# Next block's x loads, weight making and operand buffers moved between the up and down products of a Strassen-Winograd MLP pair

## The chip, the cores and the metric

The kernel runs on one core of one Trainium2 chip. The metric is the device time of one execution in microseconds (us), the median of several runs. A core has TensorE (PE: matmuls, and PEld: its weight loads), VectorE (DVE), ScalarE (ACT), GpSimd (POOL) and SyncE (SP); the last two issue nearly all DMAs here, POOL on the software queue q0, SP on the hardware queue q1.

## The reference

```
attn_out = retention(q, k, v)                      # 4 x 8 heads x 768 x 64
x = attn_out -> (3072, 512)
h = x @ w_in;  g = h * sigmoid(1.702 * h);  x = g @ w_out     # first MLP, 512 -> 2048 -> 512
h = x @ w_in2; r = max(h, 0); g = r * r;    x = g @ w_out2    # second MLP, same sizes
```

All in float32. Every operand of a big product is held as a high part and a low part (`hi`, `lo`), and a product is three matmuls: `lo*hi`, `hi*hi`, `hi*lo`.

## The kernel before

Retention comes first (24 units). Then the first MLP in its plain form for two token tiles of 512 (`for n in range(NSTD)`), and after that five *blocks* of 1024 tokens, in this order: (0, 1), which the code calls `plain`, (0, 2), (1, 0), (1, 1), (1, 2). The first number is the layer (0: first MLP, 1: second). A block has an *up* part (x times w_in) and a *down* part (g times w_out).

- The up part of `plain` is `up_plain`: 2 x 16 steps `f` of twelve matmuls, no Strassen. ScalarE applies the gelu from one of four PSUM banks (L809).
- The up part of the other blocks is `up2`: the seven products of Strassen-Winograd for each of eight `p`. An up step `p` is seven products of six matmuls each. Their results are copied (`copy`, L864, ScalarE), added (`add`, L869, VectorE) and put through gelu (layer 0) or the squared relu (layer 1: L891 and L892 on ScalarE for the quarter that needs no sum, L873 on VectorE for the three others). Products 6, 7 and 4 run on in the same PSUM bank, so each waits for the copy before it.
- The down part is `down2`: 28 steps `u` of twelve matmuls. Step u takes one operand `gx` (high and low part, made by `prepare`: L945 on ScalarE, L946 on VectorE), does one of the sums (L954, L957, L960) on g in its first twelve steps, and from step 12 on a piece (`tick`) of `x_operands`, which makes the next block's x operands (`xh`, `xl`, L702, L703). `prepare` runs two operands ahead; three pairs of tiles are used in turn, chosen by `k % 3`. Results leave through `copy` (L977), `add` (L980) and `store` (L972).

Weights of the blocks are read from DRAM (`kw`) by `fetch` (L764) on SP's queue, one tile `r` of 256 KB a product, into `SLOTS = 8` slots. Two of the slots exist early; six are opened in `up_plain` at step `f == NQ + 2` of its second half, where the pool `g` stood.

The Strassen weight combinations are made on the way by a generator, `maker`, of which `background(us)` runs pieces until their costs (the numbers that it yields) have used up the credit. A job of `make_second` loads 512 KB (`raw`, L272, POOL), scales it on ScalarE (L130, L131), joins and combines it on VectorE (L135 to L148, L377 to L381), casts it on ScalarE (L383), subtracts on VectorE (L345) and stores 896 KB (`kw<-wq`, L346, POOL). The costs of one job sum to 4.15. `later` holds a job's ScalarE pieces and its next load back until the next call of `background`. Credits: `BGK - 0.3 * c` a step of `up_plain` (c is its half), `BGUP` twice in an up step (not in the last p), `BGD` in each down step of layer 0.

The next block's x (`xb`, four tiles of 512 KB) is loaded on POOL's queue by `loads()`: in `up_plain` at `f == NQ - 2` of its second half, in `up2` at `p == NQ // 2`. POOL's queue runs in the order of the program; an xb load waits for its tile and for what stands ahead of it in that queue.

Of the kernel before, what the change touches and what calls it, by code (L numbers as in the profile page):

```python
# [11 lines left out]
F32R = mybir.dt.float32r  # L12
# [7 lines left out]
P = 128  # L20
# [6 lines left out]
NF = DFF // P  # L27
# [14 lines left out]
SLOTS = 8  # L42
EARLY = 2
BG = 4.7
BGK = 2.4
BGD = 0.35
CV0 = 12
RAWU = 7
FILL = 8
RAWS = 5  # L50
BGUP = 1.8

# [7 lines left out]
def tile_retention_then_two_ffns(  # L62
# [199 lines left out]

    raws = {}
    raw_p = []

    def load(n):
        if n < len(jobs):
# [58 lines left out]
    def make_second():  # L326

        with (
            tc.tile_pool(name="k3", bufs=1, side="right", reuse_waits="tile") as third,
            tc.tile_pool(name="k2", bufs=2, side="right", reuse_waits="tile") as pool,  # L330
        ):
            raw_p.append(third)
            load(2)
            hms = {}

            def scale(n):
                if n < len(jobs):
                    hm = raws[n][:, :, 1].bitcast(F32)
                    hms[n] = hm, later(lambda: scale_words(hm, raws[n]))

            def low(n, w, t, done):
                while not done:
                    yield None
                m, i = jobs[n]
                v.tensor_tensor(out=t[:, :, 1], in0=w[:, 1:8], in1=t[:, :, 0], op=ALU.subtract)  # L345
                nc.gpsimd.dma_start(  # L346
                    out=kw[1][m][i // 2][:, :, i % 2].rearrange("i p c -> p i c"),
                    in_=t.bitcast(F32).rearrange("p i h c -> p i (h c)"),
                )
                if i % 2:  # L350
                    made.add((1, m, i // 2))
                yield 1.1

            scale(0)
            last = None
            for n in range(len(jobs)):
                hm, done = hms.pop(n)
                while not done:
                    yield None
                scale(n + 1)  # L360
                raw = raws[n]
                hb = hm.bitcast(U32)
                w = pool.tile([P, 8, P], F32, tag="w", name=f"w32_{n}")
                wf = w.rearrange("p q c -> p (q c)")[:, 0:512]
                wu = wf.bitcast(U32)
                steps = join(wu, hb)
                next(steps)
                yield 0.45
                next(steps)
                yield 0.7  # L370
                round_up(wf, raw)
                later(lambda n=n: load(n + 3))
                yield 0.7
                if last is not None:
                    yield from low(*last)
                a21, a11, a12, a22, s1, s2, s3, s4 = (w[:, k] for k in range(8))
                v.tensor_tensor(out=s1, in0=a21, in1=a22, op=ALU.add)  # L377
                v.tensor_tensor(out=s3, in0=a11, in1=a21, op=ALU.subtract)
                yield 0.6
                v.tensor_tensor(out=s2, in0=s1, in1=a11, op=ALU.subtract)  # L380
                v.tensor_tensor(out=s4, in0=a12, in1=s2, op=ALU.subtract)  # L381
                t = pool.tile([P, 7, 2, P], F32R, tag="h", name=f"wq_{n}")
                done = later(lambda t=t, w=w: nc.scalar.copy(out=t[:, :, 0], in_=w[:, 1:8]))  # L383
                last = n, w, t, done
                yield 0.6
            yield from low(*last)
# [38 lines left out]
    hl = {}  # L425
# [15 lines left out]
    with tc.manual_schedule():  # L441
# [285 lines left out]
                lows.popleft()()  # L727
                yield

        def x_loads(l, n):  # L730
            return [load_block(f"xb{l}_{n}_{t}", (xkept, ykept)[l][2 * n + t]) for t in range(2)]


        plain = (0, NSTD // 2)
        blocks = [plain] + [(0, n) for n in range(NSTD // 2 + 1, NL)] + [(1, n) for n in range(NL)]
# [50 lines left out]
        ps_p = []  # L786
        banks = deque(range(8))

        def up_plain(loads):

            for n in range(NSTD, NSTD + 2):
                c = n - NSTD
                for f in range(NF):
                    hi, lo = weights(f, 0)
                    hp = hp_p.tile([P, TB], F32, tag="h", name=f"h{n}_{f}")
                    for k in range(KD):
                        xh, xl = hl[n][k]
                        nc.tensor.matmul(hp, lo[:, k], xh, start=(k == 0), stop=False)  # L798
                        nc.tensor.matmul(hp, hi[:, k], xh, start=False, stop=False)  # L799
                        nc.tensor.matmul(hp, hi[:, k], xl, start=False, stop=(k == KD - 1))  # L800
                    if c == 0 and f == 0:
                        down(NSTD - 1, NF - 1)
                        finish(NSTD - 1)
                        g_ctx.close()
                    r, p = divmod(f, NQ)
                    key = QS[2 * r + c], p // 2
                    if p % 2 == 0:
                        g[key] = (wa_p, wb_p)[c].tile([P, 2, TB], F32, tag="w1", name="g{}_{}".format(*key))
                    nc.scalar.activation(out=g[key][:, p % 2], in_=hp, func=ACTF.Gelu_apprx_sigmoid)  # L809
                    if c == 0 and f == 4:  # L810
                        split_x(n + 1, xs.pop(n + 1))
                    if c == 1:
                        if r == 1 and p > 0 and p % 2 == 0:
                            thirds(p // 2 - 1)
                        if f == NQ - 2:
                            loads()
                        if f in (NQ + 3, NQ + 5):
                            prepare(*plain)
                        if f == NQ + 2:
                            wr_p.extend(  # L820
                                ctx.enter_context(
                                    tc.tile_pool(name=f"wr{i}", bufs=1, side="left", reuse_waits="tile")
                                )
                                for i in range(EARLY, SLOTS)
                            )
                            fetch()
                    if f < NF - 1:
                        background(BGK - 0.3 * c)
            thirds(NQ // 2 - 1)
            first_ctx.close()  # L830
            ps_p.append(ctx.enter_context(tc.tile_pool(name="ps", bufs=1, space=PSUM, reuse_waits="tile")))
# [10 lines left out]
        def matmul(a, w, b, start, stop):  # L842
            nc.tensor.matmul(a, w, b, start=start, stop=stop, skip_group_check=True)  # L843

        def up2(l, n, first, loads):

            xb, yb, zb = {}, {}, {}
            late = deque()
# [19 lines left out]
            def add(t, a):  # L868
                v.tensor_tensor(out=t, in0=a, in1=t, op=ALU.add)  # L869
                if l == 0:  # L870
                    late.append(lambda: nc.scalar.activation(out=t, in_=t, func=ACTF.Gelu_apprx_sigmoid))
                else:
                    v.scalar_tensor_tensor(out=t, in0=t, scalar=0.0, in1=t, op0=ALU.max, op1=ALU.mult)  # L873

            for p in range(NQ + 1):
                if p == NQ // 2:
                    loads()
                if p < NQ:
                    xb[p] = bank(f"X{l}_{n}_{p}")
                    product(1, p, xb[p][0], True)  # L880
# [18 lines left out]
                        prepare(l, n)  # L899
                if p < NQ:  # L900
                    if (l, n) != blocks[-1] and p < NQ - 1:
                        background(BGUP)
                    yb = bank(f"Y{l}_{n}_{p}")
                    product(2, p, yb[0], True)
                    add(gt(11, p), yb[0])
# [6 lines left out]
                    copy(gt(22, p), xb[p][0])  # L912
                    add(gt(22, p), zb[p][0])
                    if (l, n) != blocks[-1] and p < NQ - 1:
                        background(BGUP)
                if p == NQ:
                    while late:
                        late.popleft()()
# [10 lines left out]
        def prepare(l, n):  # L929

            if not todo:
# [4 lines left out]
            hi, lo = (  # L936
                pool.tile([P, 2, TB], F32R, tag=tag, name=f"gx{l}_{n}_{i}_{m}_{e}")
                for e, (pool, tag) in enumerate(
                    ((wa_p, "w0"),) * 2 if k < 2 else
                    ((wa_p, "w0"), (wb_p, "w0")) if k % 3 == 1 else ((hl_p, "hl"),) * 2  # L940
                )
            )

# [15 lines left out]

                v.tensor_tensor(out=b11, in0=b22, in1=b11, op=ALU.subtract)  # L960

        def down2(l, n, tick):
            xb, yb, zb = {}, {}, {}
            y = {}
            last = (l, n) == blocks[-1]
# [37 lines left out]
            for i in ORDER:  # L1003
# [6 lines left out]
                for m in range(NQ // 2):  # L1010
                    gi, gm, hi, lo = ready.popleft()
                    assert (gi, gm) == (i, m)
                    u = 4 * ORDER.index(i) + m
                    if u < 12:
                        sums(u)
                    else:
                        tick()
                    prepare(l, n)
                    if l == 0:
                        background(BGD)  # L1020
                    for e in range(2):
                        a = acc[e][0]
                        for p in (2 * m, 2 * m + 1):
# [19 lines left out]
        for k, (l, n) in enumerate(blocks):  # L1043
            todo.extend((i, m) for i in ORDER for m in range(NQ // 2))
            gen = [iter(())]

            def loads():

                if k + 1 < len(blocks):
                    gen[0] = x_operands(*x_loads(*blocks[k + 1]))  # L1050

            rest = down2(l, n, lambda: next(gen[0], None))
            if (l, n) == plain:
                up_plain(loads)
            else:
                up2(l, n, rest, loads)
            for _ in rest:
                pass
            for _ in gen[0]:
                pass  # L1060
            if (l, n) == (1, 0):
                assert next(maker, 0) == 0 and not acts
# [83 lines left out]
```

## Time and profile before

| | |
|---|---|
| median of 3 runs | 1053.08 us (1051.3 to 1053.63) |
| the profiled execution | 1051.2 us, of which its span is 1049.4 us |
| TensorE busy | 1033.4 us, 98% |
| TensorE weight loads | 849.2 us, 81% |
| VectorE busy | 777.0 us, 74% |
| ScalarE busy | 531.1 us, 51% |
| DMA | 274.04 MB, mean 261 GB/s |

Times in the rows count from the start of the span. Busy shares are averages over stages; matmuls are pipelined, so that one shows as some 390 ns long while they start 227 ns apart. Idle time of TensorE is short here and lies in few places, so it is read from rows at those places. The stages begin at about 259 us (`up_plain`), 346 (its down part), 428 (up of (0, 2)), 505 (down), 585 (up of (1, 0)), 661 (down), 740 (up of (1, 1)).

### The profile page before, as it was taken

What the parts mean: (1) busy time and instruction counts of PE and PEld (TensorE: products, weight loads), DVE (VectorE), ACT (ScalarE), POOL (GpSimd) and SP (SyncE); (2) the same over time, 40 slices, a digit from 0 to 9 for tenths busy, and PEclk for the clock granted to TensorE, in tenths of its full rate; (3) what the DMA queues carried; (4) which work ended last, traced back from release to release, by engine and by line L of the source; (5) the groups of instructions that cost most, each with busy time, mean ns of one, the idle gap of its engine ahead of it and who ended that gap; (6) DMA issues with size and microseconds to landing.
All of it is one profiled execution on the core that took longest, in us unless ns stands there. A gap on an engine that the chain in (4) does not pass through costs nothing.

```text
span 1049.4 us, 15557 instructions
## 1 busy us (share of the span) xinstructions
PE 1033.4 (98%) x5602; PEld 849.2 (81%) x5602; DVE 777.0 (74%) x1083; ACT 531.1 (51%) x858; POOL 119.6 (11%) x183
## 2 busy tenths in 40 slices
PE   9999999999999899999999999999999999999998
PEld 6888888888888787887888887888788888888886
DVE  5798998798887999465799575888356986455953
ACT  4577775344765556365656334465223454233442
POOL 2221210111333101120001010000100000000000
PEclk9999999999999999999999999999999999999999
DMA  9995798856889867999787888667866667767664
GB/s 351 393 399 173 271 312 302 308 215 240 305 304 335 271 238 238 318 340 369 225 272 257 293 281 308 195 208 231 294 191 197 189 214 234 215 193 193 209 201 161
DMA packets 114637, 274.04 MB, mean 261 GB/s; under 512 B 12160, under 2 KB 12288, under 8 KB 114304
## 3 DMA queue, kind: packets, MB, share of 16 engines
q1 hardware_dynamic: 87008, 171.32, 49.6%
q0 software_dynamic: 26976, 100.67, 27.3%
q8 instruction: 45, 0.74, 0.3%
q10 hardware_dynamic: 576, 1.05, 0.3%
q14 instruction: 32, 0.26, 0.1%
HBM read 199.59 MB, written 73.40 MB: 260 GB/s over the span
## 4 chain that ended last, share of the span: by engine, by line
PE 74%; DMA 4%; DVE 3%; ACT 2%; issue 1%; POOL 0%; ACTq 0%; DVEq 0%
PE D L843 32%; PE X L843 15%; PE Z L843 8%; PE Y L843 4%; DMA r<-kw 3%; PE h L800 2%; PE h L799 2%; PE h L798 2%; PE y L676 2%; PE y L675 2%; PE y L674 2%; PE h L643 1%; PE h L644 1%; PE h L645 1%; DVE gx L946 1%
## 5 line engine op out<-in xcount | busy, mean ns | idle before, releaser
L843 PE MATMUL D<-gx,r 128*128 128x512 f32 x1680 | 385.5, 391 | 4.0 <-DVE gx L946 2.7
L843 PEld LDWEIGHTS D<-gx,r 128*128 128x128 f32 x1680 | 315.7, 188 | 72.3 <-DVE gx L946 4.6
L945 ACT CAST gx<-g 128x1024 fp32r<-128x1024 f32 x140 | 145.2, 1052 | 108.0 <-PE D L843 100.9
L946 DVE TENSOR_TENSOR gx<-g,gx 128x1024 fp32r<-128x1024 f32 x140 | 170.0, 1219 | 35.9 <-ACT gx L945 35.7
L843 PE MATMUL X<-xh,r 128*128 128x512 f32 x512 | 158.3, 390 | 1.9 <-DMA r<-kw 1.9
L864 ACT COPY g<-X 128x512 f32<-128x512 f32 x96 | 56.3, 586 | 189.9 <-PE X L843 189.9
L869 DVE TENSOR_TENSOR g<-Z,g 128x512 f32<-128x512 f32 x64 | 44.2, 690 | 133.3 <-ACT g L864 95.6
L843 PEld LDWEIGHTS X<-xh,r 128*128 128x128 f32 x512 | 95.5, 188 | 24.3 <-issue 3.8
L843 PE MATMUL X<-xl,r 128*128 128x512 f32 x256 | 99.7, 389 | 0.0
L843 PE MATMUL Z<-xh,r 128*128 128x512 f32 x256 | 79.3, 391 | 0.8 <-DMA r<-kw 0.7
L843 PEld LDWEIGHTS Z<-xh,r 128*128 128x128 f32 x256 | 47.7, 188 | 12.2 <-DMA r<-kw 1.8
L843 PEld LDWEIGHTS X<-xl,r 128*128 128x128 f32 x256 | 48.0, 188 | 10.1
L873 DVE SCALAR_TENSOR_TENSOR g<-g 128x512 f32<-128x512 f32 x72 | 49.8, 692 | 2.5
L643 PE MATMUL h<-hl,w 128*128 128x512 f32 x128 | 50.2, 392 | 0.4 <-DVE w L168 0.2
L644 PE MATMUL h<-hl,w 128*128 128x512 f32 x128 | 49.8, 389 | 0.0
L843 PE MATMUL Z<-xl,r 128*128 128x512 f32 x128 | 49.8, 389 | 0.0
L645 PE MATMUL h<-hl,w 128*128 128x512 f32 x128 | 49.8, 389 | 0.0
L676 PE MATMUL y<-gl,w 128*128 128x512 f32 x128 | 49.8, 389 | 0.0
L800 PE MATMUL h<-hl,w 128*128 128x512 f32 x128 | 49.8, 389 | 0.0
L674 PE MATMUL y<-gh,w 128*128 128x512 f32 x128 | 49.8, 389 | 0.0
L798 PE MATMUL h<-hl,w 128*128 128x512 f32 x128 | 49.8, 389 | 0.0
L675 PE MATMUL y<-gh,w 128*128 128x512 f32 x128 | 49.8, 389 | 0.0
(105 smaller groups left out, 1588.9 us busy)
## 6 DMA issues: line engine op xcount, KB each, us to landing
r<-kw SPq DMA_DIRECT2D x504, 256.0 KB, 2.9
kw<-wq POOLq DMA_DIRECT2D x32, 896.0 KB, 6.5
unit<-qkv SPq DMA_DIRECT2D x48, 512.0 KB, 9.2
raw<-w POOLq DMA_DIRECT2D x32, 512.0 KB, 6.0
kw<-wh POOLq DMA_DIRECT2D x16, 1024.0 KB, 4.7
kw<-w SPq DMA_DIRECT2D x16, 512.0 KB, 4.9
raw<-win POOLq DMA_DIRECT2D x16, 512.0 KB, 7.0
raw<-wout POOLq DMA_DIRECT2D x16, 512.0 KB, 6.5
```

What stands on the lines that cost most here:

```text
L643: nc.tensor.matmul(hp, lo[:, k], xh, start=(k == 0), stop=False)
L644: nc.tensor.matmul(hp, hi[:, k], xh, start=False, stop=False)
L645: nc.tensor.matmul(hp, hi[:, k], xl, start=False, stop=(k == KD - 1))
L674: nc.tensor.matmul(a, lo[:, e], gh, start=s0, stop=False)
L675: nc.tensor.matmul(a, hi[:, e], gh, start=False, stop=False)
L676: nc.tensor.matmul(a, hi[:, e], gl, start=False, stop=s1)
L798: nc.tensor.matmul(hp, lo[:, k], xh, start=(k == 0), stop=False)
L800: nc.tensor.matmul(hp, hi[:, k], xl, start=False, stop=(k == KD - 1))
L843: nc.tensor.matmul(a, w, b, start=start, stop=stop, skip_group_check=True)
L864: nc.scalar.copy(out=t, in_=a)
L945: nc.scalar.copy(out=hi, in_=src)
L946: v.tensor_tensor(out=lo, in0=src, in1=hi, op=ALU.subtract)
```

## The change

- `loads(u)`: the xb loads are written into steps 0 to 3 of the down part, one tile a step, instead of in the up part.
- `background(BGD)` is gone from the down part. `BGUP` becomes a pair, 2.15 in layer 0 and 2.4 in layer 1 (before 1.8); `BGK` becomes 2.6 with `- 0.2 * c` (before 2.4 and 0.3). The last three steps of `up_plain`'s second half call no `background`.
- `up_plain` prepares three operands (at NQ + 1, NQ + 3, NQ + 5) instead of two, the first three from `wa`; step 0 of its down part prepares none.
- A third buffer `k4` for `wq` (every third job) stands from the closing of pool `g` to `f == NQ + 4` of the second half, where now the six slots are opened.
- In block (1, 0) the squared relu of the three summed quarters is a Relu and a Square on ScalarE, put behind the next copy, instead of one instruction of VectorE.

```
-BGK = 2.4
-BGD = 0.35
+BGK = 2.6
...
-BGUP = 1.8
+BGUP = (2.15, 2.4)
...
-                t = pool.tile([P, 7, 2, P], F32R, tag="h", name=f"wq_{n}")
+                t = (spare[0] if spare and n % 3 == 2 else pool).tile([P, 7, 2, P], F32R, tag="h", name=f"wq_{n}")
...
                         g_ctx.close()
+                        spare.append(g_ctx.enter_context(
+                            tc.tile_pool(name="k4", bufs=1, side="left", reuse_waits="tile")
+                        ))
...
-                        if f == NQ - 2:
-                            loads()
-                        if f in (NQ + 3, NQ + 5):
+                        if f in (NQ + 1, NQ + 3, NQ + 5):
                             prepare(*plain)
-                        if f == NQ + 2:
+                        if f == NQ + 4:
+                            spare.clear()
+                            g_ctx.close()
...
-                    if f < NF - 1:
-                        background(BGK - 0.3 * c)
+                    if f < NF - 1 - 3 * c:
+                        background(BGK - 0.2 * c)
...
                 if l == 0:
                     late.append(lambda: nc.scalar.activation(out=t, in_=t, func=ACTF.Gelu_apprx_sigmoid))
+                elif n == 0:
+                    late.append(lambda: nc.scalar.activation(out=t, in_=t, func=ACTF.Relu))
+                    late.append(lambda: nc.scalar.activation(out=t, in_=t, func=ACTF.Square))
                 else:
                     v.scalar_tensor_tensor(out=t, in0=t, scalar=0.0, in1=t, op0=ALU.max, op1=ALU.mult)
...
-                if p == NQ // 2:
-                    loads()
...
-                        background(BGUP)
+                        background(BGUP[l])
...
-                    ((wa_p, "w0"),) * 2 if k < 2 else
-                    ((wa_p, "w0"), (wb_p, "w0")) if k % 3 == 1 else ((hl_p, "hl"),) * 2
+                    ((wa_p, "w0"),) * 2 if k < 3 else
+                    ((wa_p, "w0"), (wb_p, "w0")) if k % 3 == 2 else ((hl_p, "hl"),) * 2
...
+                    if u < 4:
+                        loads(u)
                     if u < 12:
                         sums(u)
                     else:
                         tick()
-                    prepare(l, n)
-                    if l == 0:
-                        background(BGD)
+                    if u > 0 or (l, n) != plain:
+                        prepare(l, n)
...
+            def loads(u):
...
+                if i == 0:
+                    xt.append(block_tiles(f"xb{b}_{j}_{t}"))
+                nc.gpsimd.dma_start(out=xt[t][i], in_=(xkept, ykept)[b][2 * j + t][:, 2 * i:2 * i + 2])
+                if u == 3:
+                    gen[0] = x_operands(*xt)
```

GpSimd's queue at the end of the up part of (0, 2), before. `raw` and `kw` are the maker's loads and stores, `xb` the next block's x.

```order
L346 DMA kw_105<-wq_4673 128x7x256
L689 DMA xb_0_0_0_4763<-ykept_113 128x1024
L689 DMA xb_0_0_1_4764<-ykept_113 128x1024
L689 DMA xb_0_1_0_4767<-ykept_114 128x1024
L689 DMA xb_0_1_1_4768<-ykept_114 128x1024
L346 DMA kw_106<-wq_4759 128x7x256
L272 DMA raw_26_4846<-wout 128x1024
L346 DMA kw_106<-wq_4852 128x7x256
```

The same place of the change (`o` is the down part's first result).

```order
L346 DMA kw_106<-wq_4862 128x7x256
L272 DMA raw_26_4941<-wout 128x1024
L346 DMA kw_106<-wq_4947 128x7x256
L1059 DMA xb_0_0_0_5077<-ykept_113 128x1024
L1059 DMA xb_0_0_1_5078<-ykept_113 128x1024
L1059 DMA xb_0_1_0_5144<-ykept_114 128x1024
L1059 DMA xb_0_1_1_5145<-ykept_114 128x1024
L973 DMA ykept_117<-o_2_11_5180 128x512 x2
```

The xb loads stand behind the last maker store of the up part, with no maker's transfer between them and the down part's first store.

VectorE from the second operand of the plain block (`gx_1_1_1_1`) to the third (`gx_1_1_2_1`), before; `w` and `wq` are a maker's tiles, L836 a third, L954 a sum.

```order
L946 TENSOR_TENSOR gx_1_1_1_1_3728<-g_1_3049,gx_1_1_1_0_3727 128x1024
L345 TENSOR_TENSOR wq_3708<-w_15_3659,wq_3708 128x7x128
...
L380 TENSOR_TENSOR w_16_3709<-w_16_3709 128x128
L381 TENSOR_TENSOR w_16_3709<-w_16_3709 128x128
L135 TENSOR_SCALAR w_17_3759<-raw_17_3600 128x512
L140 SCALAR_TENSOR_TENSOR w_17_3759<-raw_17_3600,w_17_3759 128x512
L148 SCALAR_TENSOR_TENSOR w_17_3759<-w_17_3759,raw_17_3600 128x512
L836 TENSOR_TENSOR g_3_3519<-g_3_3753,g_3_3519 128x1024
L954 TENSOR_TENSOR g_0_2997<-g_0_3384,g_0_2997 128x1024
L946 TENSOR_TENSOR gx_1_1_2_1_3787<-g_2_3095,gx_1_1_2_0_3786 128x1024
```

The same of the change, to the first sums.

```order
L947 TENSOR_TENSOR gx_1_1_1_1_3666<-g_1_3053,gx_1_1_1_0_3665 128x1024
L380 TENSOR_TENSOR w_16_3624<-w_16_3624 128x128
L381 TENSOR_TENSOR w_16_3624<-w_16_3624 128x128
L134 TENSOR_SCALAR w_17_3674<-raw_17_3568 128x512
L139 SCALAR_TENSOR_TENSOR w_17_3674<-raw_17_3568,w_17_3674 128x512
L147 SCALAR_TENSOR_TENSOR w_17_3674<-w_17_3674,raw_17_3568 128x512
L836 TENSOR_TENSOR g_1_3446<-g_1_3640,g_1_3446 128x1024
L947 TENSOR_TENSOR gx_1_1_2_1_3744<-g_2_3101,gx_1_1_2_0_3743 128x1024
L836 TENSOR_TENSOR g_2_3493<-g_2_3691,g_2_3493 128x1024
L836 TENSOR_TENSOR g_3_3543<-g_3_3760,g_3_3543 128x1024
L955 TENSOR_TENSOR g_0_3000<-g_0_3396,g_0_3000 128x1024
```

The third operand stands ahead of two thirds and of the first sum now, and the maker's last pieces end before it.

ScalarE in one up step of (1, 0), from the copy of product 1 of `p` 3 to the next `p`, before.

```order
L864 COPY g_1_3049<-X_0_3_6001 128x512
L891 ACTIVATE g_1_3249<-X_0_2_5916 128x512
L892 ACTIVATE g_1_3249<-g_1_3249 128x512
L864 COPY g_1_3429<-X_0_3_6001 128x512
L864 COPY g_1_3619<-X_0_3_6001 128x512
```

The same of the change.

```order
L864 COPY g_1_3053<-X_0_3_5973 128x512
L873 ACTIVATE g_1_3640<-g_1_3640 128x512
L874 ACTIVATE g_1_3640<-g_1_3640 128x512
L892 ACTIVATE g_1_3261<-X_0_2_5880 128x512
L893 ACTIVATE g_1_3261<-g_1_3261 128x512
L383 CAST wq_5968<-w_27_5912 128x7x128
...
L864 COPY g_1_3446<-X_0_3_5973 128x512
L873 ACTIVATE g_1_3446<-g_1_3446 128x512
L874 ACTIVATE g_1_3446<-g_1_3446 128x512
L873 ACTIVATE g_1_3053<-g_1_3053 128x512
L874 ACTIVATE g_1_3053<-g_1_3053 128x512
L864 COPY g_1_3640<-X_0_3_5973 128x512
```

Six instructions of the squared relu came to ScalarE, four of them between the second copy and the third.

## Rows read from the trace of the kernel before

**Rows 1.** The page's first part: busy us, share of the span, instructions.

```profile
PE 1033.4 (98%) x5602; PEld 849.2 (81%) x5602; DVE 777.0 (74%) x1083; ACT 531.1 (51%) x858; POOL 119.6 (11%) x183
```

**Rows 2.** The chain that ended last: start us, us, what ran or was waited for.

```profile
470.63 12.39 DMA r<-kw
483.07 1.67 PE Z L843 x6
...
505.13 2.72 PE D L843 x12
...
631.13 11.48 DMA r<-kw
642.75 1.62 PE X L843 x6
...
743.88 9.68 DMA r<-kw
753.60 1.65 PE Z L843 x6
```

**Rows 3.** Timeline of TensorE around the plain block's third down step.

```profile
351.32 0.84 PE L843 MATMUL D<-gx,r 128*128 128x512 f32 x3
354.90 4.46 PE L843 MATMUL D<-gx,r 128*128 128x512 f32 x12 [2.74 <-DVE gx L946]
```

**Rows 4.** Busy times of a stretch behind that wait, PEclk the granted clock.

```profile
355.00:358.40 3.40, 3.40 (x9) 2.69 (x10) 3.40 (x4) 0.00 (x0) 0.00 (x0) 0.55 0.63 224
```

**Rows 5.** Waits of TensorE over the span: us in total, times, longest.

```profile
PE D L843 <- ACT o L977: 1.3, 2, 0.9
```

**Rows 6.** Timeline of GpSimd, whose instructions here issue DMAs.

```profile
322.99 2.19 POOL L689 DMA_DIRECT2D xb<-xkept  x4
...
462.21 2.13 POOL L689 DMA_DIRECT2D xb<-ykept  x4
470.77 0.95 POOL L346 DMA_DIRECT2D kw<-wq  x1 [6.43 <-DVE wq L345]
471.71 0.58 POOL L272 DMA_DIRECT2D raw<-wout  x1
...
625.30 2.18 POOL L689 DMA_DIRECT2D xb<-ykept  x4
633.27 0.95 POOL L346 DMA_DIRECT2D kw<-wq  x1 [5.79 <-DVE wq L345]
...
741.33 2.12 POOL L689 DMA_DIRECT2D xb<-ykept  x4
```

**Rows 7.** Busy times of two down parts: plain block, block (1, 0).

```profile
346.30:428.40 82.10, 78.41 (x337) 63.74 (x336) 73.20 (x82) 43.69 (x51) 9.07 (x14) 0.98 0.76 252
...
660.70:739.80 79.10, 79.10 (x350) 65.28 (x349) 63.45 (x59) 39.75 (x44) 3.64 (x7) 1.00 0.68 213
```

**Rows 8.** Timeline of ScalarE near the end of the plain up part.

```profile
335.98 0.66 ACT L130 ACTIVATE raw<-raw 128x512 f32<-128x512 f32 x1 [4.57 <-DMA raw<-win]
336.55 0.66 ACT L131 ACTIVATE raw<-raw 128x512 uint32<-128x512 uint32 x1
```

**Rows 9.** DMA queues from 625 to 640 us: packets, MB, share of 16 engines.

```profile
q0 software_dynamic: 955, 3.58, 69.4%
q1 hardware_dynamic: 817, 1.49, 28.9%
```

**Rows 10.** The page's DMA issues: count, KB each, median us to landing.

```profile
r<-kw SPq DMA_DIRECT2D x504, 256.0 KB, 2.9
```

**Rows 11.** Groups by line over the span: busy us, mean ns of one.

```profile
L864 ACT COPY g<-X 128x512 f32<-128x512 f32 x96 | 56.3, 586 | 189.9 <-PE X L843 189.9
L873 DVE SCALAR_TENSOR_TENSOR g<-g 128x512 f32<-128x512 f32 x72 | 49.8, 692 | 2.5
L383 ACT CAST wq<-w 128x896 fp32r<-128x896 f32 x32 | 30.1, 940 | 13.9 <-DMA kw<-wq 8.3 <-DVE w L381 2.4 <-issue 1.8
L892 ACT ACTIVATE g<-g 128x512 f32<-128x512 f32 x24 | 15.2, 632 | 0.8
```

More of the change, by code (lines that the diff above doesn't have):

```diff
@@ L264, in tile_retention_then_two_ffns @@
     raw_p = []
+    spare = []
     def load(n):
@@ L728, in x_operands @@
                 yield
-        def x_loads(l, n):
-            return [load_block(f"xb{l}_{n}_{t}", (xkept, ykept)[l][2 * n + t]) for t in range(2)]
         plain = (0, NSTD // 2)
@@ L787, in tile_retention_then_two_ffns, with up_plain @@
         banks = deque(range(8))
-        def up_plain(loads):
+        def up_plain():
             for n in range(NSTD, NSTD + 2):
@@ L843, in matmul, with up2 @@
             nc.tensor.matmul(a, w, b, start=start, stop=stop, skip_group_check=True)
-        def up2(l, n, first, loads):
+        def up2(l, n, first):
             xb, yb, zb = {}, {}, {}
@@ L914, in up2 @@
                     if (l, n) != blocks[-1] and p < NQ - 1:
-                        background(BGUP)
+                        background(BGUP[l])
                 if p == NQ:
@@ L960, in sums, with down2 @@
                 v.tensor_tensor(out=b11, in0=b22, in1=b11, op=ALU.subtract)
-        def down2(l, n, tick):
+        def down2(l, n, loads, tick):
             xb, yb, zb = {}, {}, {}
@@ L1045, in tile_retention_then_two_ffns @@
             gen = [iter(())]
[L1047 to L1052, printed above, removed]
+            xt = []
+            def loads(u):
+                if k + 1 == len(blocks):
+                    return
+                t, i = divmod(u, 2)
+                b, j = blocks[k + 1]
+                if i == 0:
[3 more added lines that the diff above has]
+                    gen[0] = x_operands(*xt)
+            rest = down2(l, n, loads, lambda: next(gen[0], None))
             if (l, n) == plain:
-                up_plain(loads)
+                up_plain()
             else:
-                up2(l, n, rest, loads)
+                up2(l, n, rest)
             for _ in rest:
```

## The prediction, made before the run

> **What bounds the kernel now.** I read the page's busy times first: TensorE is busy for 98% of the span [rows 1], so the change can only give back TensorE's idle or slowed time. Where that lies is read from the waits of TensorE and from the chain that ended last, after the attention stage (which the change leaves alone). A product, six 128x512 matmuls, takes 1.36 us when nothing is late: twelve take 2.72 [rows 2]. Two kinds of loss stand against this.
>
> **Late operands.** In the plain block's down products the third step starts at 354.90. The three matmuls before it begin at 351.32 and would hand over 0.68 us later, at 352.00: 2.90 us are lost, and VectorE's gx is what came last [rows 3]. The twelve matmuls then take 4.46 us, not 2.72 plus 0.16 for the modelled end of the last: 1.58 more. In that stretch the granted clock is 0.55 [rows 4], near the lower of the two levels (1.2 GHz), after an idle stretch; it is back behind it. Two more waits in down products, for ScalarE's copy of a finished bank, hold 1.3 us [rows 5]; with 0.16 of pipeline each, 1.6. Sum: 4.5 + 1.6 = 6.1 us.
>
> **Late weights.** r tiles live in 8 slots. One is fetched again when its product ends, and is needed seven products, 9.52 us, later. The chain shows three places where the DMA took longer: 470.63 to 483.07 (12.44), 631.13 to 642.75 (11.62), 743.88 to 753.60 (9.72), each followed by a product of 1.62 to 1.67 rather than 1.36 [rows 2]. Lost: 2.92+0.31, 2.10+0.26, 0.20+0.29, in all 3.2+2.4+0.5 = 6.1 us. Just before each, GpSimd's queue issued the four xb loads, 2.1 MB [rows 6]. So about 12.2 us can be had, 1.2% of the span.
>
> **The change, step by step.**
>
> *Rest in the down products.* BGD = 0.35 in 28 steps of both first-layer down blocks gave 2 x 28 x 0.35 = 19.6 us of making to VectorE there. In the plain block's down products VectorE is busy 73.2 of 82.1 us; in the next layer's, which never had making, 63.5 of 79.1, and TensorE is busy for all 79.10 [rows 7]. Taking the making out turns the first into the second: I price the two copy waits at nothing afterwards. Gain 1.6. The bound from below is 0, if the late copies come from the x operands alone.
>
> *Third buffer, third early prepare, no making in the last three steps.* ScalarE stood 4.57 us for raw<-win at 335.98 [rows 8], because the xb loads had been issued just ahead of it at 322.99 [rows 6]; its gx casts ran late, and VectorE then did the third operand after two thirds and a sum. In the new order that operand precedes them, three making steps fewer stand ahead, and xb comes behind the last raw. All of the 4.5 should go. What could keep it: the six late r slots, now behind the k4 buffer's last store (job 14, issued about six steps before the products begin at 346.3, so some 16 us ahead). Bounds 1.4 (only the idle half goes) and 4.5; I take 4.5, since both causes named in the rows leave. For the extra buffer itself I take nothing: a wait of ScalarE here has four PSUM banks, 10.9 us, of cover.
>
> *The x loads.* In the text they move to steps 0 to 3 of the down products. But nothing on GpSimd's queue makes them wait for those steps: what stands ahead is the last maker's load or store, or the last output store, and the tiles are free by then. In the plain block they go out behind the last raw load, about 337 to 340, when no r competes: harmless. In block (0, 2) they now follow the store of job 23, issued some 3 us into the last up step, with no maker behind. In (1, 0) they follow the store of job 31, likewise. In (1, 1) the rows ahead and behind are the same as before, so its 0.5 stays. So most of the burst is kept, and what shrinks is the maker traffic around it. Lost time against what was queued at once (2.1 MB of xb, 0.92 a kw store, 0.52 a raw load, 0.26 an output store): 2.6 MB lost 0.5 us, 3.9 MB lost 2.4, 4.5 MB lost 3.2, about 1.4 us per MB [rows 2, 6]. Now (1, 0) has 3.0 MB: 1.1; (0, 2) has 3.0 and a raw load half a step earlier, 3.5: 1.8; (1, 1) 0.5. In all 3.4 for 6.1: gain 2.7. Bounds: 0 (kept as it is) and 6.1 (spread as the text reads).
> While such a burst lasts, the software queue moved 3.58 MB and the r queue 1.49 MB in 15 us, 29% for r [rows 9]: 99 GB/s where the products eat 193 (262 KB per 1.36 us). By the Trainium skill, DMA: Bandwidth & Descriptors, section Queues, rings and completion order, each DMA engine goes round robin between queues, a packet at a time. Were that equal shares of bytes, r would get 169 GB/s and lose 0.36 MB in such 15 us, 1.9 us of its reserve of 6.6 (9.52 less the 2.9 that a fetch takes [rows 10]): by that rule no burst would stop TensorE, and 6.1 us of waits say that here it isn't equal bytes.
>
> *More making in the up products.* A job costs 4.15 us in the code's own credits. With 4.3 per up step in (0, 2) one comes every 9.2 us, with 4.8 in (1, 0) every 8.2 (before: 3.6 and 11.0). Each moves 1.44 MB while raws last. At the software queue's 239 GB/s [rows 9] that is 6.0 us, in which r falls behind by 0.56 MB; made up at some 200 GB/s above its need, that is 2.8 us: a period of 8.8 us holds. (0, 2) is above it; (1, 0) is 0.6 below for five jobs, so r grows late by up to 3 us of its reserve. I take 0.5 us for it, between 0 and 3.
>
> *Squared relu of block (1, 0).* 24 times one VectorE instruction of 692 ns becomes two on ScalarE of 632. An up step has 9.52 us. On ScalarE it now holds three copies (1.76), four pairs (5.06) and 1.16 jobs of two scalings and a cast (1.16 x (2 x 0.66 + 0.94) = 2.6): 9.4 us by durations [rows 8, 11]. But ScalarE's instructions overlap: 0.66 long, they start 0.57 apart [rows 8]. So some 8.2 us, 86%. The tight places are the copies that a product waits for, with 1.36 us of cover; ahead of the second stand four of the new instructions, 2.2 us, in the 2.72 that it has. I take 0.5 us for late operands or stores there, between 0 and 5 (0.7 a step).
> The Trainium skill, ScalarE: Activation LUTs, section Rules for kernel authors, says to put relu, max and mul on VectorE and not on ScalarE. By duration the row agrees (1.26 for 0.69); by that rule this part only costs, and its price is the third rival's.
>
> **Sum.** 1.6 + 4.5 + 2.7 - 0.5 - 0.5 = 7.8 us. The profiled execution took 1051.2 (span 1049.4 and 1.8 around it): 1043.4. The median of the runs shown, 1053.1, lies 1.9 above it, so for a median 1045.3.
>
> **The rivals.**
> *All r waits go* (0.14): bursts of 3.0 MB stay inside the 9.52 us, as the maker's chunks of 1.44 MB do. Gain 1.6+4.5+5.6-0.5 = 11.2: 1041.9. Against it: 2.6 MB alone still lost 0.5.
> *The plain block's stall stays in part* (0.11), because r or the third operand is late for another reason: 3 us back, 1048.3.
> *ScalarE becomes the bound in (1, 0)* (0.12): from 9.52 us of real occupation per up step on. Each step then stops twice at a copy, 0.7 us a step, 5 us in all: 1050. For it, the 9.4 by durations; against it, the overlap.
> *Makers starve r, and the kernel is slower* (0.05). Place: up products of (0, 2) and (1, 0). Seven steps need 49 r tiles, 12.9 MB, and 10.4 and 10.0 MB of making, in 66.7 us: 349 and 342 GB/s, where the burst moved 5.07 MB in 15 us, 338 [rows 9]. It decides once the DMA moves less than about 340 over the whole stage. At 320 the stages take 72.8 and 71.3, 10.7 more, and the bursts at their end find no reserve, so that 6.1 stays lost: 1053.1 - 6.1 + 10.7 = 1057.7.
> My forecast has the remaining 0.58.
>
> **How the numbers follow.** The forecast's own range is 1042.5 to 1048 (x loads between 0 and 6.1 of gain, 3 us for makers). With the rivals' first three the range is 1040 to 1050.5; it leaves out the slower case and some of the others' tails. Within 0.2% of 1053.1 (1051 to 1055.2, about what a measurement of this kernel can tell from no change) would need several of the costs together: 0.07. Slower 0.04, faster 0.89.
>
> **What would show it.** The plain block's third down step without an idle stretch and without a low clock; no wait for ScalarE's o copies; xb issued in one run behind the last kw store, ahead of the down products; waits for r<-kw still there at the end of the up products of (0, 2) and (1, 0), some 3 us together, and the one after (1, 1)'s start unchanged. I'd be wrong if xb loads stood apart by 2.7 us, if r waits grew in the middle of the up products, or if TensorE waited there for ScalarE's g copies.

## The result, and the profile after

Changed kernel: median 1041.74 us of 6 runs (1041.35 to 1044.67); kernel before, beside it: 1052.21 of 6 (1047.24 to 1053.79). Ratio 0.9911, 95% interval [0.9887, 0.9936]. The profiled execution took 1041.52 us with a span of 1039.8, against 1051.2 and 1049.4. The forecast was 1043.4 for this execution and 1045.3 for the median, with a range of 1040.0 to 1050.5.

The page of the changed kernel, its busy times and the granted clock in 40 slices:

```profile
PE 1028.8 (99%) x5602; PEld 849.1 (82%) x5602; DVE 762.5 (73%) x1059; ACT 559.1 (54%) x906; POOL 119.7 (12%) x183
...
PEclk9999999999999999999999999999999999999999
```

Against [rows 1], ScalarE took over 28 us of work and VectorE gave 14.5 off. No slice shows a lower clock, nor did one before: a slice is 26 us long, and the slowed stretch of [rows 4] some 3. The two longest waits of TensorE over the span (us in total, times, longest):

```profile
PE D L843 <- DMA r<-kw: 2.9, 4, 1.0
PE sc L487 <- DMA unit<-qkv: 1.4, 4, 0.5
...
```

The second and the three shorter ones left out lie in the first 165 us, in the attention stage, what leads up to it and the start of the first MLP; behind that there is only the first. The waits for gx and for ScalarE's o copies [rows 3, 5] are gone. In the chain that ended last, these pieces answer to [rows 2]:

```profile
345.13 76.33 PE D L843 x336
...
492.21 10.23 DMA r<-kw
...
646.51 10.78 DMA r<-kw
```

The plain block's 56 down products now take 76.33 us in one piece, 1.363 each: nothing is late. Two of the three late fetches of r remain, each now at the start of a down part, and the one of block (1, 1) is gone. TensorE at those two places (idle time before a group and its releaser in brackets):

```profile
499.95 0.39 PE L843 MATMUL Z<-xl,r 128*128 128x512 f32 x1
500.52 0.96 PE L843 MATMUL D<-gx,r 128*128 128x512 f32 x3 [0.19 <-DMA r<-kw]
502.48 0.73 PE L843 MATMUL D<-gx,r 128*128 128x512 f32 x2 [0.99 <-DMA r<-kw]
...
654.25 0.39 PE L843 MATMUL Z<-xl,r 128*128 128x512 f32 x1
655.38 0.96 PE L843 MATMUL D<-gx,r 128*128 128x512 f32 x3 [0.75 <-DMA r<-kw]
657.33 5.05 PE L843 MATMUL D<-gx,r 128*128 128x512 f32 x21 [0.98 <-DMA r<-kw]
```

A matmul of these starts 0.227 us after the one ahead. From start to start, (0, 2) loses 0.34 and 1.28 us and (1, 0) 0.90 and 1.27; with 0.1 of smaller steps, 1.7 and 2.3. Taken in this way over all such matmuls behind the attention stage (steps of 0.02 us and more), the loss fell from 13.0 us to 4.5. I use this measure below as "lost in the trace". GpSimd at the issue of xb, in place of [rows 6]:

```profile
338.33 2.16 POOL L1059 DMA_DIRECT2D xb<-xkept  x4
...
488.78 0.94 POOL L346 DMA_DIRECT2D kw<-wq  x1 [7.27 <-DVE wq L345]
489.72 2.18 POOL L1059 DMA_DIRECT2D xb<-ykept  x4
...
642.85 0.94 POOL L346 DMA_DIRECT2D kw<-wq  x1 [7.25 <-DVE wq L345]
643.78 2.15 POOL L1059 DMA_DIRECT2D xb<-ykept  x4
...
732.07 2.12 POOL L1059 DMA_DIRECT2D xb<-ykept  x4
```

All four loads leave in one run, directly behind whatever stands last on GpSimd's queue: a maker's store in (0, 2) and (1, 0), an output store for the last. That is 5 us ahead of the down part's first step in (1, 0) (649.0), and 72 us in (1, 1) (804.0). Busy times of the down parts of [rows 7], and of the up products of (0, 2) and (1, 0) (columns PE, PEld, DVE, ACT, POOL, then the granted clock, DMA share, GB/s):

```profile
346.30:428.40 82.10, 82.10 (x363) 67.75 (x362) 62.66 (x61) 39.77 (x47) 5.83 (x10) 1.00 0.74 240
660.70:739.80 79.10, 79.10 (x350) 65.33 (x349) 58.57 (x55) 37.33 (x42) 6.45 (x12) 1.00 0.71 228
581.00:649.00 68.00, 68.00 (x301) 56.21 (x300) 45.12 (x81) 58.94 (x100) 11.93 (x16) 1.00 0.96 335
428.40:495.00 66.60, 66.60 (x296) 55.14 (x295) 43.68 (x78) 42.18 (x73) 12.21 (x17) 1.00 1.00 351
```

TensorE stands still in none of the four. VectorE in the plain down part fell from 73.20 to 62.66.

### The profile page after: what moved, and what is told of

Read it like the earlier page. It is cut to its first block, busy times and chain, and to the rows that moved or that the text cites. A ratio compares the mean times of both kernels' runs of the same rounds, so it can differ in the third digit from the quotient of the medians.

```text
span 1039.8 us, 15581 instructions
## 1 busy us (share of the span) xinstructions
PE 1028.8 (99%) x5602; PEld 849.1 (82%) x5602; DVE 762.5 (73%) x1059; ACT 559.1 (54%) x906; POOL 119.7 (12%) x183
## 4 chain that ended last, share of the span: by engine, by line
PE 82%; DMA 2%; DVE 0%; issue 0%
PE D L843 36%; PE X L843 16%; PE Z L843 8%; PE Y L843 4%; PE h L797 3%; PE h L795 3%; PE h L796 3%; DMA r<-kw 2%; PE y L676 2%; PE y L674 2%; PE y L675 2%; PE h L643 2%; PE h L645 1%; PE h L644 1%; DVE o L981 0%
## 5 line engine op out<-in xcount | busy, mean ns | idle before, releaser
L643 PE MATMUL h<-hl,w 128*128 128x512 f32 x128 | 50.2, 392 | 0.4 <-DVE w L167 0.4
L644 PE MATMUL h<-hl,w 128*128 128x512 f32 x128 | 49.9, 390 | 0.0
L645 PE MATMUL h<-hl,w 128*128 128x512 f32 x128 | 49.8, 389 | 0.0
L795 PE MATMUL h<-hl,w 128*128 128x512 f32 x128 | 49.8, 389 | 0.0
L796 PE MATMUL h<-hl,w 128*128 128x512 f32 x128 | 49.8, 389 | 0.0
L797 PE MATMUL h<-hl,w 128*128 128x512 f32 x128 | 49.8, 389 | 0.0
```

## The experiments

**Theory A**: what is left, 4 us, comes from the xb burst, because nothing paces the loads; and most of the 13.0 was burst and late operands. **Rival B**: makers, or the software queue as such, keep r late. **Rival C**: the parts that I priced at nothing or little carry the gain. The kernels ran in three groups, each on one chip with runs of the kernel before beside it (first group: 1050.70 of 19 runs).

**The x loads issued by SyncE.** The r fetches are issued there, each behind the product that frees its slot.

```diff
-                nc.gpsimd.dma_start(out=xt[t][i], in_=(xkept, ykept)[b][2 * j + t][:, 2 * i:2 * i + 2])
+                nc.sync.dma_start(out=xt[t][i], in_=(xkept, ykept)[b][2 * j + t][:, 2 * i:2 * i + 2])
```

> The changed kernel with its four xb loads a block issued on SyncE's queue, between the fetches of r, in place of GpSimd's. My theory: in the changed kernel nothing on GpSimd's queue paces these loads, so all four leave at once and hold r up at 500 and 655 us (about 4 us of TensorE's time together). On SyncE's queue an xb load stands behind r fetches that wait for their slots, so one leaves per down step: r lands within 9.5 us everywhere, TensorE has no wait for r, and the time falls by 3.5 to 4 us against the changed kernel, to about 1038. The rival, that the DMA engines are simply full there whoever issues: the same waits on r, in other places, 1041 to 1042.

1037.78 us (4 runs, 1037.48 to 1038.75), ratio 0.9884 [0.9865, 0.9902]. SyncE in the down part of (0, 2):

```profile
496.02 0.37 SPq L1059 DMA_DIRECT2D xb<-ykept  x1
497.64 3.72 SPq L761 DMA_DIRECT2D r<-kw  x4
501.54 0.32 SPq L1059 DMA_DIRECT2D xb<-ykept  x1
...
506.90 0.37 SPq L1059 DMA_DIRECT2D xb<-ykept  x1
```

The first load leaves at 496.02 and the fourth at 506.90, with r fetches between, and TensorE waits for r nowhere. The 4 us came back, as theory A says; but queue and pacing changed together.

**The x loads back in the up products**, all else of the change kept.

```diff
+                        if f == NQ - 2:
+                            for u in range(4):
+                                loads(u)
...
+                if p == NQ // 2:
+                    for u in range(4):
+                        loads(u)
...
-                    if u < 4:
-                        loads(u)
```

> The changed kernel with the xb loads put back to their old places in the up products (step 6 of the plain block's second half; p = 4 of the others). My theory: with the denser making, 3.9 to 4.5 MB stand in the queue again and r is late by 3 us in (0, 2) and 2.5 in (1, 0) in the middle of the up products, against 1.7 and 2.3 at their end; (1, 1) as it was; in the plain block ScalarE waits some 4 us for a raw load again, but the third early operand and the rest in the last three steps cover it, so at most 1 us is lost there. In all 2 to 4 us more than the changed kernel: 1044 to 1046. The rival, that the place of the loads was the whole gain: 8 us more, 1050. The other rival, that it did nothing: within 1 us of 1041.7.

1044.43 (8 runs, 1042.56 to 1048.33), ratio 0.995 [0.9933, 0.9966]. That is in the expected range. In the profiled run, the fastest of the eight, the r waits are back in the middle of the up products, 2.8 us lost in (0, 2) and 1.5 in (1, 0). The plain block is the surprise of detail. GpSimd issues the burst there as before:

```profile
322.22 2.15 POOL L1063 DMA_DIRECT2D xb<-xkept  x4
```

And ScalarE's timeline has its old wait for a raw load behind it again (3.91 us, for 4.57 in [rows 8]):

```profile
337.81 0.68 ACT L129 ACTIVATE raw<-raw 128x512 f32<-128x512 f32 x1 [3.91 <-DMA raw<-wout]
```

Yet TensorE loses only 0.1 us there. With the third operand prepared early, less making ahead of it and the third `wq` buffer, ScalarE's wait costs nothing; this run does not split the three.

**The mirror: before, with only the x loads moved** to the down steps, on GpSimd.

```diff
-                            loads()
...
+                    if u < 4:
+                        loads(u)
...
+                nc.gpsimd.dma_start(out=xt[t][i], in_=(xkept, ykept)[b][2 * j + t][:, 2 * i:2 * i + 2])
```

> The kernel before with one part of the change alone: the xb loads written into down steps 0 to 3. My theory: the raw load in the plain block no longer stands behind xb, so ScalarE's 4.57 us wait goes and the stall at 354.9 falls from 4.5 us to between 0 and 1.5; the two waits for ScalarE's o copies (1.6 us) stay; r is late by 2 to 3 us in all after the up products, since the bursts are still whole. Gain 4 to 6 us: 1046 to 1048. The rival, that the rest and the operand buffer did it: the stall at 354.9 stays above 3 us, and the time stays within 2.5 us of the kernel before.

1045.11 (12 runs, 1043.43 to 1050.96), ratio 0.9957 [0.9941, 0.9972], a little better than expected. The profiled execution, 1048.18, is one of the longer ones. The plain stall shrinks from 4.5 to 0.9 us. So either remedy alone, xb out of the way or the operand parts, takes most of it; the o copies keep their 1.2. The r waits are not the 2 to 3 us that I expected: in this execution (0, 2) alone loses 6.1, as much as the three places together before, while (1, 0) and (1, 1) lose 0.4 each. TensorE's timeline in (0, 2):

```profile
505.15 0.96 PE L839 MATMUL D<-gx,r 128*128 128x512 f32 x3 [1.09 <-DMA r<-kw]
507.71 8.58 PE L839 MATMUL D<-gx,r 128*128 128x512 f32 x24 [1.60 <-DMA r<-kw]
```

Busy times in a stretch behind these waits (columns as above):

```profile
509.00:512.00 3.00, 3.00 (x8) 2.32 (x8) 1.61 (x3) 0.47 (x1) 0.00 (x0) 0.50 0.21 72
```

Two waits hold 2.7 us, and the rest of the 6.1 is mainly 13 matmuls 427 ns apart, with the clock granted at 0.50.

**The squared relu of (1, 0) back on VectorE.**

```diff
-                elif n == 0:
-                    late.append(lambda: nc.scalar.activation(out=t, in_=t, func=ACTF.Relu))
-                    late.append(lambda: nc.scalar.activation(out=t, in_=t, func=ACTF.Square))
```

> The changed kernel with block (1, 0)'s squared relu of the three summed quarters back on VectorE as one instruction. My theory: ScalarE had room (no wait of TensorE for it in the changed kernel), VectorE too, so TensorE's time does not change: within 0.5 us of the changed kernel, 1041 to 1042.5. The rival, that VectorE is too full for this with the denser making: sums of Z and Y run late in the up products of (1, 0), TensorE waits for VectorE or for a copy there, 2 us or more on top, 1044.

1041.94 (6 runs, 1040.07 to 1043.86), ratio 0.9923 [0.9906, 0.994], and no wait for either engine in that up part:

```profile
581.00:649.00 68.00, 68.00 (x302) 56.33 (x301) 58.26 (x102) 35.66 (x58) 11.53 (x16) 1.00 0.96 334
```

ScalarE 35.66 and VectorE 58.26, instead of 58.94 and 45.12, and TensorE full in both. Its profiled execution, the slowest of the six, loses 3.8 us to r in (0, 2), where the change lost 1.7. That part is worth nothing in either direction.

**Before, with only the x loads moved, on SyncE** (the diff of the mirror with `nc.sync`). Second group of runs, before 1050.75.

> The kernel before with the xb loads alone changed: written into down steps 0 to 3 and issued on SyncE's queue. None of the change's other parts. My theory: waits for r go entirely (6.1 us), the raw load at 336 no longer waits behind xb, so the plain block's stall falls to between 0 and 1; the two waits for o copies (1.6 us) stay. 1050.7 less 9.5 to 10.5: 1040 to 1041, so faster than the changed kernel. The rival, that the rest of the makers and the operand buffer carry the gain: 1043 or more.

1041.03 (6 runs, 1039.92 to 1042.31), ratio 0.9911 [0.9895, 0.9928]: this one edit gives what the whole change gives, and is not told apart from it. No r wait is left; 0.6 us of gx and 1.2 of o copies remain. The three kernels that follow undo parts of the change, the second of them several at once, with x on SyncE, against the 1037.78 of the first experiment.

**Making back in the first layer's down products.**

```diff
+                    if l == 0:
+                        background(0.35)
```

> The changed kernel with x on SyncE's queue, and with the making of 0.35 a step back in the down products of the first layer. It stands against the run with x on SyncE's queue, 1037.8. My theory: VectorE is full in the first twelve steps again, the x operands and so ScalarE's o copies come late at the end of products 7, and TensorE waits 1 to 2 us in all for ScalarE's o: 1039 to 1040. The rival, that those waits came from the late start of the plain block's down part and not from the making: no wait for o, within 0.5 us of 1037.8.

1041.36 (6 runs, 1041.06 to 1042.39), ratio 0.9915 [0.9901, 0.9929]; 3.5 us more lost in the trace. The waits that came:

```profile
PE D L843 <- ACT o L978: 1.3, 2, 1.1
...
PE D L843 <- DVE gx L947: 0.8, 2, 0.5
```

Right in direction, larger than the 1 to 2 expected: the making makes gx late too, not only o.

**Two early operands, the old buffers for them, and making up to the last step.**

```diff
-                        if f in (NQ + 1, NQ + 3, NQ + 5):
+                        if f in (NQ + 3, NQ + 5):
...
-                    if f < NF - 1 - 3 * c:
+                    if f < NF - 1:
...
-                    ((wa_p, "w0"),) * 2 if k < 3 else
-                    ((wa_p, "w0"), (wb_p, "w0")) if k % 3 == 2 else ((hl_p, "hl"),) * 2
+                    ((wa_p, "w0"),) * 2 if k < 2 else
+                    ((wa_p, "w0"), (wb_p, "w0")) if k % 3 == 1 else ((hl_p, "hl"),) * 2
```

> The changed kernel with x on SyncE's queue, with two early operands in place of three, the buffers as before, and making in the last three steps of the plain up part again. My theory: once xb no longer stands ahead of the raw loads, ScalarE is not late and the old two operands nearly do: TensorE waits 0 to 1 us for gx in the plain block's down part, 1037.8 to 1039. The rival, that these parts took the 4.5 us stall away: 2.5 us or more come back, 1040 or more.

1041.39 (6 runs, 1039.56 to 1042.54), ratio 0.9914 [0.9898, 0.9931]; 2.3 lost in the plain block, at one wait:

```profile
353.00 5.30 PE L843 MATMUL D<-gx,r 128*128 128x512 f32 x22 [2.04 <-DVE gx L947]
```

I had expected 0 to 1, since the same parts lost only 0.9 in the kernel before once xb was out of the way. VectorE shows what stands ahead of it here:

```profile
348.85 0.69 DVE L139 SCALAR_TENSOR_TENSOR w<-raw,w 128x512 uint32<-128x512 uint32 x1
349.46 1.22 DVE L836 TENSOR_TENSOR g<-g,g 128x1024 f32<-128x1024 f32 x1
350.59 1.22 DVE L955 TENSOR_TENSOR g<-g,g 128x1024 f32<-128x1024 f32 x1
351.73 1.22 DVE L947 TENSOR_TENSOR gx<-g,gx 128x1024 fp32r<-128x1024 f32 x1
```

A maker's unpacking, the last third and a sum stand ahead of the operand, back to back, with no wait among them. That the denser making is why these parts count for more here is my reading; no run has them with the old credits.

**Without the third wq buffer.**

```diff
-                t = (spare[0] if spare and n % 3 == 2 else pool).tile([P, 7, 2, P], F32R, tag="h", name=f"wq_{n}")
+                t = pool.tile([P, 7, 2, P], F32R, tag="h", name=f"wq_{n}")
```

> The changed kernel with x on SyncE's queue and without the third buffer for wq. My theory: ScalarE waits longer for kw stores in the plain up part, as it did for 8.3 us before, but four PSUM banks cover it: within 0.5 us of 1037.8. The rival, that with a job every 4.3 us two buffers no longer do: the delays add up to the end of the stage and cost 1.5 us or more at the start of the down part.

1040.05 (5 runs, 1038.91 to 1041.96), ratio 0.9902 [0.9885, 0.9919]. TensorE waits for gx in the plain block, and 1.2 us are lost. TensorE's timeline:

```profile
355.79 2.58 PE L843 MATMUL D<-gx,r 128*128 128x512 f32 x10 [0.93 <-DVE gx L947]
```

ScalarE's cast of a maker's tile shows where it comes from:

```profile
327.92 0.95 ACT L383 CAST wq<-w 128x896 fp32r<-128x896 f32 x1 [2.50 <-DMA kw<-wq]
```

It stands for the store that empties its buffer; the wait delays gelu and the casts of gx behind it in the same queue. Over the plain up part ScalarE's casts wait 15.9 us for such stores, in 8 waits, and not at all in the first experiment, with the third buffer. There the first three casts of gx start at 330.05, 335.83 and 340.93, here at 336.82, 342.58 and 344.48. My expectation of no loss was wrong, and rival C right for this part.

**Paced on GpSimd.** Last group, before 1050.93. Each xb load is put behind a copy, on GpSimd, of one column of `g[11, u]`, which VectorE's sums write in that step; the copy is extra work and its result isn't used.

```diff
+                    if u < 4:
+                        nc.gpsimd.tensor_copy(out=pace[:, u:u + 1], in_=g[11, u][:, 0, 0:1])
+                        loads(u)
```

> The changed kernel with the xb loads still on GpSimd's queue, but each behind a copy of one column of the sum of its down step (g 11 of step u), so that GpSimd waits for VectorE's sum of that step. My theory: what cost r its time in the changed kernel is that the four loads leave at once behind the last kw store. One load per down step, on the same software queue, leaves r in time: TensorE waits for r 0 to 0.5 us in all, 1037.5 to 1038.5, like x on SyncE's queue. The rival, that the software queue itself holds r up, and that SyncE's queue helped since it is r's own: the waits for r stay at 2 us or more, 1040 to 1042.

1038.15 (4 runs, 1037.24 to 1041.38), ratio 0.988 [0.9861, 0.9899]. No r wait; GpSimd:

```profile
498.13 1.05 POOL L1019 COPY pad<-g 128x1 f32<-128x1 f32 x1 [7.78 <-DVE g L956]
499.12 0.59 POOL L1061 DMA_DIRECT2D xb<-ykept  x1
...
505.87 0.55 POOL L1061 DMA_DIRECT2D xb<-ykept  x1
```

Same queue as in the change, same bytes, only later and apart: so when and how close together the loads leave is the cause, and rival B falls. Which of the two counts, later or apart, no run splits.

**The x loads issued by ScalarE** (`nc.scalar`).

> The changed kernel with the xb loads issued by ScalarE, a hardware queue that r does not use; they stand among its gx casts, which wait for TensorE. My theory: paced like on SyncE's queue, so no wait for r; issuing costs ScalarE some 0.5 us each in steps where it has room: 1037.5 to 1038.5. The rival, that only r's own queue keeps the order: waits for r stay, 1040 or more.

1038.72 (4 runs, 1037.25 to 1040.56), ratio 0.9881 [0.9864, 0.9898], no r wait. In (0, 2) the loads leave at 497.93, 504.10 (two) and 505.86 us. A third engine whose queue is held by the step's work gives the same.

**Making in the last three up steps of the plain block again**, third operand kept, x on SyncE.

```diff
-                    if f < NF - 1 - 3 * c:
+                    if f < NF - 1:
```

> The changed kernel with x on SyncE's queue and with making in the last three steps of the plain up part again; the third early operand stays. It splits the run with both undone, which lost 2.3 us at the start of the plain block's down part. My theory: the third operand stands ahead of the thirds on VectorE and takes most of it away, so 0 to 1 us is lost there: 1038 to 1039. The rival, that the rest in the last steps was what counted: 1.5 us or more come back, 1040.

1040.24 (5 runs, 1039.55 to 1042.73), ratio 0.9901 [0.9884, 0.9918]. 1.8 us are lost at one place in TensorE's timeline:

```profile
348.86 3.47 PE L843 MATMUL D<-gx,r 128*128 128x512 f32 x14 [1.57 <-ACT g L809]
```

ScalarE ahead of it:

```profile
345.20 0.95 ACT L383 CAST wq<-w 128x896 fp32r<-128x896 f32 x1 [2.33 <-DMA kw<-wq]
...
347.09 0.67 ACT L129 ACTIVATE raw<-raw 128x512 f32<-128x512 f32 x1 [0.45 <-DMA raw<-wout]
...
348.22 0.58 ACT L809 ACTIVATE g<-h 128x512 f32<-128x512 f32 x1
```

The last gelu stands behind a maker's cast and two scalings, so the rival won: rest in the last steps counts. I had expected 0 to 1.

**The changed kernel once more**, beside these three.

> The changed kernel once more, beside the others on one chip. 1041 to 1042.5, with 3.5 to 4.5 us of waits for r at the start of the down parts of (0, 2) and (1, 0).

1043.43 (5 runs, 1042.09 to 1044.36), ratio 0.9922 [0.9908, 0.9936]; 2.9 us lost in (0, 2), 1.6 in (1, 0). That is above the 1041 to 1042.5 that I expected. Its interval lies above those of both paced forms on the same chip.

## Why the prediction was right, point by point

**What bounds it.** Right. 9.6 us of span were given back: 8.5 of the 13.0 lost behind the attention stage. The other 1.1 is no gain of the change: the matmuls behind the attention stage begin at 82.7 us in place of 83.8, and the change leaves that stage alone. There the wait for unit loads ran from 0.4 to 3.7 us over the kernels' profiles.

**The x loads.** The mechanism is shown: not paced, one run behind the last store, the r waits at the ends of (0, 2) and (1, 0). The forecast kept 3.4 us lost (1.8, 1.1, 0.5); the profile shows 4.0 (1.7, 2.3, 0), and the second run of the same kernel 4.6 (2.9, 1.6, 0.1). The rule of 1.4 us per MB gave the sum and not the parts. In (1, 1) the rows ahead and behind xb are as before, and the 0.5 went all the same; it is 0 to 0.1 in each profile with the change's other parts, and 0.4 in the mirror, but from what, no run tells. Each profile with the four loads issued together loses 4.0 to 6.8 us at these three places, and none with them apart more than 0.6. The rule that each DMA engine takes turns between queues, a packet at a time (the Trainium skill, DMA: Bandwidth & Descriptors, section Queues, rings and completion order), I had read as equal bytes, by which no burst stops TensorE. By packets the trace agrees with it: in [rows 9] 955 to 817, nearly equal turns. But a packet of the software queue held 3.7 KB there and one of r's queue 1.8, so r got 29% of the bytes. At those 99 GB/s, where 193 are eaten, r falls 1.4 MB behind in 15 us; that is 7.3 us, more than the reserve of 6.6 that I gave it.

**The plain stall.** All 4.5 us went, as forecast. Its causes were not a sum, though: moving xb alone took 3.6 of it, and with xb left in place the operand parts took all but 0.1. ScalarE's wait for raw, which I named as its origin, is back in that run and costs nothing.

**Rest in the down products.** The two o waits went; this is the 1.6. But the term was priced from the making of before. Put back into the changed kernel with x on SyncE, the making costs 3.6 by medians.

**The third wq buffer, "I take nothing".** This step failed: without it 1.2 us are lost in the trace, and the median is 2.3 higher (the profiled executions differ by 1.7, of which 0.5 lies in the attention stage). The cover that I gave it, four PSUM banks, is for products; the wait sits on ScalarE's queue ahead of gelu and of casts whose operand is due in the first down steps.

**More making, -0.5.** The strain came, the cost did not. The up products now move 351 and 335 GB/s, against the 349 and 342 of the rival that starves r. The 2.9 that a fetch of r takes [rows 10] is a median over the whole span. In the middle of the up products, with no xb load near, a fetch took 4.5 us in (0, 2) before (435 to 460 us) and takes 5.1 now. In (1, 0), from 590 to 620 us, before and after:

```profile
r<-kw SPq DMA_DIRECT2D x22, 256.0 KB, 3.8
...
r<-kw SPq DMA_DIRECT2D x22, 256.0 KB, 5.3
```

That is inside the 9.52 us which it has, and no wait came of it. It also shows that the reserve of 6.6 us, worked out from 2.9, was too large.

**Squared relu, -0.5.** ScalarE is at 58.94 of 68.00, 87%, where I had worked out 86%, and no copy is late: 0. The page that I weighed against it (the Trainium skill, ScalarE: Activation LUTs, section Rules for kernel authors) keeps relu, max and mul on VectorE; with them there the time was 1041.94, with ScalarE 1041.74, so here neither engine is the better place.

**The sum.** The late operands gave their 6.1, the loads 2.1 for 2.7, both costs were 0 for 1.0, and steps too small for the list of waits gave 0.3: 8.5. With 1.1 from the attention stage, which is luck, it is the 9.6 of span, where 7.8 had been forecast. The median came out 3.6 below its forecast of 1045.3: 1.9 of it is this, and 1.7 comes from the step from the profiled execution to the median, 1.9 before and only 0.2 after. The rival in which all r waits go came near the measured time (1041.9) by the wrong way: 4.0 us of them are still there.

## What to carry to other kernels

In these kernels a place in the program's text delays a transfer only if something ahead of it on its engine's queue waits there: read what stands before it, and where nothing does, issue it from a queue that the step's own work holds, or hang it on a value of that step. Here this alone is worth what the whole change is, and both together 1037.78 us, ratio 0.9884, the lowest median of this study. What a part is worth depends on what stands beside it. With x on SyncE, taking out the rest in the down products, the rest in the last up steps and the extra buffer, one at a time, costs 3.6, 2.5 and 2.3 us by medians, 8.4 together; yet the kernel before, which has none of them, loses only 3.3 against the same kernel (1041.03 for 1037.78). That the denser making is what makes them needed is argued: no run has it alone, and none takes out the third early operand alone.

## What the runs showed of the hardware that was not expected

How much a late r costs depends on whether the clock falls behind it, and the idle time alone doesn't say when. In the second run of the changed kernel, TensorE's timeline at its longest wait:

```profile
504.00 3.02 PE L843 MATMUL D<-gx,r 128*128 128x512 f32 x12 [1.86 <-DMA r<-kw]
```

Behind it, in the same run, the granted clock (the column ahead of the last two):

```profile
504.20:506.20 2.00, 2.00 (x10) 1.60 (x10) 2.00 (x2) 0.05 (x1) 0.00 (x0) 1.00 1.04 392
```

The same place in the kernel with the relu on VectorE:

```profile
504.24 4.04 PE L843 MATMUL D<-gx,r 128*128 128x512 f32 x11 [1.96 <-DMA r<-kw]
```

And its clock behind that wait:

```profile
504.40:508.00 3.60, 3.60 (x11) 2.86 (x12) 3.26 (x3) 0.96 (x1) 0.00 (x0) 0.65 0.90 312
```

The first keeps the full clock (1.00 is 2.4 GHz), the second pays 1.6 us more for eight matmuls 427 ns apart, and the 1.60 after 1.09 of the mirror run pays for 13. It isn't simply that the second is longer: the 2.04 us wait for gx of the kernel with two early operands (353.00) is longer still, and behind it the granted clock is 1.00 from 353.2 to 358.0. What decides it stays open.
